# Sliding-window attention into a two-layer network: some transposes moved from TensorE to DMA, and the first steps reordered

## The chip, the cores and the metric

The kernel runs on one core of one Trainium2 chip. The metric is the device time in microseconds of one execution. The profile shows one execution of the program, recorded by the hardware profiler.

Engine names in the views: PE is TensorE's matrix multiplication, PEld its weight load, DVE is VectorE, ACT is ScalarE, POOL is GpSimd, SP is SyncE, which here only issues DMAs. A name such as SPq is the instruction queue of that engine.

## What is computed

```python
batch, n_heads, seq, head_dim = (8, 8, 576, 64)          # q, k, v in float32
n_tokens, d_model, d_ff = (4608, 512, 2048)

# attention: each query sees itself and the 63 keys before it
scores = scale * np.matmul(q, k.transpose(0, 1, 3, 2))
rel = pos[:, None] - pos[None, :]
mask = (rel >= 0) & (rel < 64)
attn = softmax(np.where(mask, scores, -1e9))
attn_out = np.matmul(attn, v)

# heads side by side, then two layers
x = attn_out.transpose(0, 2, 1, 3).reshape(B * S, H * D)   # 4608 x 512
h = x @ w_in
g = h - np.tanh(h)
out = g @ w_out                                            # float32
```

## The kernel before

**Units.** A batch has 576 tokens, that is 9 windows of 64. Two heads make a pair, so a batch has 4 pairs; the number g counts the 32 pairs over all batches (g = 4 b + pair). The two layers work on chunks of 512 tokens, 8 windows, so there are 9 chunks, and a chunk can need windows of two batches: chunk c needs the windows 8c to 8c + 7 of all 72, batch b makes the windows 9b to 9b + 8.

**One pair.** Loads on POOL's queue bring q, k and v of a batch into SBUF and turn them to bf16 on the way; the first loads come in float32 by the queues of ACT and SP. `cast` copies a pair into rows of 128 (two heads side by side), on POOL for most pairs. `tr` transposes 6 such blocks of 96 rows on TensorE into PSUM (L197); the result is copied into `qT` by ACT and VectorE (two copies of 64 partitions) or into `kT` by one copy. `scores` multiplies keys by queries, 9 windows in three groups of three (L210); for the first 8 pairs a second matmul adds the mask (L213). ACT takes the exponential of each group into `PT`. From pair 8 on VectorE multiplies `PT` by the mask (`masking`, L218). `pv` multiplies by v, which has a column of ones for the sum (L224). `norm` divides by that sum on VectorE (L231, L235) and writes `xs`, tokens on partitions. The scores of two heads lie side by side in one matmul, since `qT` holds each head's queries with zeros in place of the other's.

**v.** `cast_v` copies v into `vb`; nine small DMAs (`keys_v`) put each window's keys into the upper 64 partitions of `vw`, and `shift_v` copies them one window on into the lower 64, by VectorE for the first two batches and by one DMA on SP's queue (L135) for the others.

**x.** The layers need x with the model dimension on partitions. `x_tr` transposes 4 or 5 windows of a batch for one half of its heads on TensorE (L241) into PSUM, and ACT or VectorE copies them into `xT`, the tile of a chunk:

```python
o = chunk_tile(c).rearrange("p (h r) (w t) -> p r h w t", r=2, t=64)
```

**The layers.** `hp_mm` multiplies one block of 128 hidden units by the chunk (4 matmuls of 512 columns, L259), ACT takes the tanh (L262), and `g_sub` subtracts it on VectorE and writes `gT` (L268). `yp_mm` multiplies `gT` by `w_out` (L278), 4 matmuls at a time; ACT copies a finished 128 x 512 block and SP stores it (L283, L285).

**The order.** Everything is put on the engines' queues in the order in which the program is written; the engines run their queues in order and wait for one another on semaphores. Slots h order it: an even slot holds one `hp_mm` step, an odd slot one `yp_mm` step, 16 steps behind. After each of them the slot's other work is issued. Chunk c begins at slot 32 c. For the pairs from 12 on this work is laid out by a formula: pair g begins at slot a = 8 g - 48.

```python
at(a - 7, cast, g, "q")
at(a - 5, cast, g, "k")
at(a, tr, g, "q", 3, nc.scalar, nc.vector)
at(a + 2, tr, g, "k", 3, nc.scalar)
for i in range(3):
    at(a + 5 + 2 * i, scores, g, i, 4)
at(a + 11, masking, g)
```

For the first 12 pairs it is written by hand in `PLAN`: a script for each slot, and one (slot -1) for all that goes ahead of the first layer step. A word of a script is a step, its numbers and its engines (a ACT, v VectorE, p POOL, s SP): E and F are `tr` of q and k, a and b their casts, R is a group of scores, P is `pv` with `norm`, M `masking`, X `x_tr` (batch, half of the heads, part), d the cast of v, k `keys_v`, z `shift_v`, q and r loads of one pair, Q, K and V loads of a batch, w and o loads of the weights, i, m and n constants.

**PSUM.** Banks 0 and 1 take the first layer, 2 the second, 3 the transposes, 4 the scores, 5 to 7 the products with v.

Of the kernel before, what the change touches and what calls it, by code (L numbers as in the profile page):

```python
# [7 lines left out]
F32 = mybir.dt.float32  # L8
BF16 = mybir.dt.bfloat16
# [6 lines left out]
def kernel(  # L16
# [9 lines left out]
    nc = tc.nc  # L26
    B, H, S, D = q.shape
    NP = H // 2
    NJ = S // 64
    E, P = 6, S // 6  # L30
# [4 lines left out]
    TOK = 512  # L35
    WPC = TOK // 64
# [4 lines left out]
    ctx.enter_context(tc.manual_schedule())  # L41

    const = ctx.enter_context(tc.tile_pool(name="const", bufs=1))
    qk_pool = ctx.enter_context(tc.tile_pool(name="qk", bufs=2))
    all_pool = ctx.enter_context(tc.tile_pool(name="all", bufs=2))
    v_pool = ctx.enter_context(tc.tile_pool(name="v", bufs=1))
    row_pool = ctx.enter_context(tc.tile_pool(name="row", bufs=3))
    sm_pool = ctx.enter_context(tc.tile_pool(name="sm", bufs=3))
    xt_pool = ctx.enter_context(tc.tile_pool(name="xt", bufs=3))
    g_pool = ctx.enter_context(tc.tile_pool(name="g", bufs=2))  # L50
    psum = ctx.enter_context(tc.tile_pool(name="psum", bufs=1, space=PSUM))


# [10 lines left out]
    NR, NPT = 2, 4  # L64
# [5 lines left out]
    PT = [const.tile([128, NJ, 128], BF16, name=f"pt{i}") for i in range(NPT)]  # L70
    kT = [const.tile([128, 64 + S], BF16, name=f"kt{i}") for i in range(NR)]
    qT = [const.tile([128, 2, S], BF16, name=f"qt{i}") for i in range(NR)]
    xs = [const.tile([128, NJ, NP, D], BF16, name=f"xs{i}") for i in range(2)]

    stage, rows, whole = {}, {}, {}

    def move(eng, o, i):
        if eng is nc.scalar:
            nc.scalar.activation(o, i, ACT.Copy)  # L79
        else:  # L80
            eng.tensor_copy(o, i)  # L81

    def load(g, n, eng):

        b, pr = divmod(g, NP)
        if eng is nc.gpsimd:
            if (b, n) not in whole:
                whole[b, n] = all_pool.tile([P, H, E * D], BF16, tag=n, name=n + "all")
            t = whole[b, n][:, pr::NP]
        else:  # L90
            t = qk_pool.tile([P, 2, E * D], F32, tag=n + "f", name=n + "f")
        eng.dma_start(out=t, in_=(q if n == "q" else k)[b, pr::NP].rearrange("h (p e) d -> p h (e d)", e=E))
        stage[g, n] = t

# [49 lines left out]
    def w_in_tile(ki, m):  # L144
        i = min(m // 4, 2)
        f = 512 * (m // 4 - i) + m % 4
        return w_in_sb[i][:, ki, f:f + 4 * 127 + 1:4]
# [14 lines left out]
    def more_constants():  # L162
        nc.vector.memset(qT[1], 0.0)
        nc.vector.memset(kT[1][:, 0:64], 0.0)
        for i in range(2):
            nc.vector.memset(vw[i][0:64, 0], 0.0)

        for h in range(2):  # L170
            nc.gpsimd.memset(hide[:, h], 0.0)
            nc.gpsimd.affine_select(hide[:, h], hide[:, h], compare_op=ALU.is_ge, fill=-(2.0 ** 30),
                                    base=-1, pattern=[[-1, 64]], channel_multiplier=1)
            nc.gpsimd.affine_select(hide[:, h], hide[:, h], compare_op=ALU.is_ge, fill=-(2.0 ** 30),
                                    base=64, pattern=[[1, 64]], channel_multiplier=-1)
# [9 lines left out]
    xT = {}  # L185

    def chunk_tile(c):
        if c not in xT:
            xT[c] = xt_pool.tile([128, 4, TOK], BF16, tag="xT", name="xT")
        return xT[c]  # L190


    def tr(g, which, bank, *engs):
# [9 lines left out]
        else:  # L203
            move(engs[0], kT[g % NR][:, 64:].rearrange("c (p e) -> c p e", e=E), t)

    def scores(g, grp, bank):
        sp = ps[:, bank, 0:384].rearrange("p (i q) -> p i q", i=3)
        for i in range(3):
            j = 3 * grp + i
            nc.tensor.matmul(sp[:, i, :], kT[g % NR][:, 64 * j:64 * j + 128],  # L210
                             qT[g % NR][:, :, 64 * j:64 * j + 64], start=True, stop=g >= 2 * NP)
            if g < 2 * NP:
                nc.tensor.matmul(sp[:, i, :], ident, hide.rearrange("p h t -> p (h t)"), start=False, stop=True)  # L213
        nc.scalar.activation(PT[g % NPT][:, 3 * grp:3 * grp + 3, :], sp, ACT.Exp, scale=scale)  # L214
# [23 lines left out]
    def x_tr(b, half, w0, w1, bank, eng=nc.vector):  # L238
        tp = ps[:, bank, :].bitcast(BF16)[:, 0:640].rearrange("p (w t) -> p w t", t=128)
        for w in range(w0, w1):  # L240
            nc.tensor.transpose(tp[:, w - w0, :],  # L241
                                xs[b % 2][:, w, 2 * half:2 * half + 2, :].rearrange("p r d -> p (r d)"), ident)
        lo, hi = b * NJ + w0, b * NJ + w1
        while lo < hi:
            c = lo // WPC
            to = min(hi, (c + 1) * WPC)
            o = chunk_tile(c).rearrange("p (h r) (w t) -> p r h w t", r=2, t=64)
            i0 = lo - b * NJ - w0
            move(eng, o[:, half, :, lo - c * WPC:to - c * WPC],
                 tp[:, i0:i0 + to - lo].rearrange("p w (h t) -> p h w t", h=2))  # L250
            lo = to


# [2 lines left out]
    def hp_mm(c, m):  # L256
        hp = ps[:, m % 2, :]
        for ki in range(4):
            nc.tensor.matmul(hp, w_in_tile(ki, m), chunk_tile(c)[:, ki, :],  # L259
                             start=(ki == 0), stop=(ki == 3))  # L260
        th = sm_pool.tile([128, TOK], F32, tag="th", name="th")
        nc.scalar.activation(th, hp, ACT.Tanh)  # L262
        return hp, th
# [27 lines left out]
    def at(h, *fn):  # L291
        items.setdefault(h, []).append(fn)
# [13 lines left out]
    def play(script):  # L306
        for step in script.split():
            what = step[0]
            n = [int(i, 36) for i in step[1:] if i not in "apvs"]
            eng = [ENG[i] for i in step[1:] if i in "apvs"]  # L310
            if what in "qr":
                load(*n, "q" if what == "q" else "k", *eng)
            elif what in "QK":
                load_all(*n, what.lower())
# [41 lines left out]

    PLAN = {
        -1: """
            q0a i v00 a0v v02 v03 v01 d00v d02a r0s b0a r1p q1a E0vv r2p m d03p F0a d01v q3p
            R01 b2a k05s b1a a1v k00s k08a k01p k02a R02 k04a k06s F1a E1vv q2p V1 a2v R00 R12 K1  # L360
            a3p n k07s F2a Q1 k03s z0v w0 d13p w1 K2 E2aa R11 P0 r3s R10 b3a b5p E3va P1
            R21 b6p w2 b4p Q2 d10p F3v a4p R20 d11p R22 P2 V2 d12a k17s k12s k16s k10s R30 k18s
            b7p o3 R32 R31 X001v a7p o2 P3 X010v o0 a5p X000v X011a E4vv a9p b8p""",
        0: "F4a",
        10: "R40 k13s F5v k15s E5aa R42 a6v k14s aAp k11s",
        12: "a8p d20p R41 d23p d21p d22p z1v k24s E6av F6a k27s R50 k25s b9p o1 P4",
        15: "R51 R52 R61 F7a k22s P5 R62 bAp R60 E7va",
        16: "k21p",
        19: "bBp P6 X100a R71 k20s k28s F8a k23s k26s R70",
        20: "R72 E8vv",  # L370
        23: "X101a z2s R80 E9aa P7 R81",
        26: "F9a R82 X111a X110a",
        31: "R90 EAvv",
        35: "M8 R92 FAa aBv R91 FBa M9 RA2",
        41: "P9 RA0 EBaa",
        44: "P8 RB0",
        50: "RA1 MA X200a RB1 X201v PA RB2",
        56: "MB PB",
        60: "X210v",
        62: "X211a",  # L380
# [4 lines left out]

    for g in range(3 * NP, B * NP):
        b, pr = divmod(g, NP)
        a = 8 * g - 48
        at(a - 7, cast, g, "q")
        at(a - 5, cast, g, "k")  # L390
        at(32 * b - 72 + 5 * pr, cast_v, b, pr)
        at(a, tr, g, "q", 3, nc.scalar, nc.vector)
        at(a + 2, tr, g, "k", 3, nc.scalar)
        for i in range(3):
            at(a + 5 + 2 * i, scores, g, i, 4)
        at(a + 11, masking, g)
        for i in range(3):
            at(a + 13 + i, pv, g, i)
        at(a + 15, norm, g)
        if pr % 2 == 1:  # L400
            at(a + 20, x_tr, b, pr // 2, 0, 4, 3)
            at(a + 22, x_tr, b, pr // 2, 4, NJ, 3)
        for j in range(NJ):
            if pr == 0:
                at(32 * b - 54 + j // 2, keys_v, b, j)
        if pr == 0:
            at(32 * b - 78, load_v_all, b)
            at(32 * b - 64, load_all, b, "q")
            at(32 * b - 63, load_all, b, "k")
            at(32 * b - 47, shift_v, b, 0, NJ - 1)  # L410

    LAG = 16
    for h in range(min(items), 2 * (16 * NC + LAG) + 2):
        n = h // 2
        c, m = divmod(n, M)
        cy, sy = divmod(n - LAG, M)
        if h % 2 == 0:
            if sy % 4 == 0 and 0 < n - LAG <= 16 * NC:
                y_out(*divmod((n - LAG) // 4 - 1, 4))
            if 0 <= c < NC:  # L420
                hidden = hp_mm(c, m)
        elif 0 <= cy < NC:
            yp_mm(cy, sy)
        for fn in items.get(h, []):
            fn[0](*fn[1:])
        if h % 2 == 0 and 0 <= c < NC:
            g_sub(c, m, *hidden)
# [29 lines left out]
```

The softmax here doesn't subtract the row's maximum and nothing guards it: scores larger than these inputs give would overflow.

## Time and profile before

| | |
|---|---|
| time, median of 11 runs | 363.42 us (361.31 to 366.63) |
| the profiled execution: time | 362.93 us |
| the profiled execution: span from first to last instruction | 361.2 us |
| mean granted TensorE clock | 0.993 |
| busy: TensorE, VectorE, ScalarE, GpSimd | 323.4, 215.3, 192.8, 103.8 us |
| DMA | 36.76 MB, mean 102 GB/s |
| first layer: 552 matmuls recorded | 146.2 us, 382 ns each |
| second layer: 559 matmuls recorded | 143.0 us, 379 ns each |
| transposes of q, of k, of x on TensorE | 192, 192, 144 matmuls; 14.4, 14.7, 13.1 us |

In the rows of the page and of the views below, a group's row gives the line in the kernel, the engine, the operation, output and inputs by their names, the shape and the number of instructions. The time of a matmul in the trace runs from its start to its modelled end, and matmuls overlap, so that start-to-start distances say what one costs. The slices of the page are 40 equal parts of the span, about 9 us each, with the busy share in tenths.

### The profile page before, as it was taken

How to read it: one execution, taken by the hardware profiler on the slowest of the kernel's cores; microseconds unless marked ns; L12 is line 12 of the kernel's file. 1: busy time of each engine (PE TensorE's matmuls, PEld its weight loads, DVE VectorE, ACT ScalarE, POOL GpSimd, SP SyncE). 2: the span in 40 equal slices, each digit the busy share in tenths (PEclk: the TensorE clock that was granted, in tenths of full speed). 3: DMA queues.
4: the chain of work that ended last, by engine and by line, in shares of the span. 5: the costliest groups of instructions: out<-in, count | busy, mean ns of one | idle time of the engine just before them, and what ended most of it. 6: DMA issues, size and time to landing. Idle time of an engine off the chain costs nothing.

```text
span 361.2 us, 6002 instructions
## 1 busy us (share of the span) xinstructions
PE 323.4 (90%) x2288; PEld 189.0 (52%) x2329; DVE 215.3 (60%) x352; ACT 192.8 (53%) x355; POOL 103.8 (29%) x136
## 2 busy tenths in 40 slices
PE   0528687889999999999999999999999999999995
PEld 0427345655555555555555555555555544444442
DVE  4317667865676776767777767767666633443300
ACT  3435366876566656565655565655664444444421
POOL 7708353806318408402730372110000000000000
PEclk9999899999999999999999999999999999999999
DMA  8899993467876576755935591250000010010012
GB/s 163 138 214 186 214 221 64 59 132 133 196 141 92 89 164 112 148 104 127 136 79 112 135 138 54 62 123 31 30 32 29 31 58 29 31 58 29 31 68 78
DMA packets 31948, 36.76 MB, mean 102 GB/s; under 512 B 3472, under 2 KB 25872, under 8 KB 31536
## 3 DMA queue, kind: packets, MB, share of 16 engines
q0 software_dynamic: 20384, 17.90, 32.9%
q1 hardware_dynamic: 10904, 17.69, 17.0%
q10 hardware_dynamic: 632, 0.79, 0.7%
q8 instruction: 18, 0.29, 0.3%
q14 instruction: 10, 0.08, 0.1%
HBM read 36.70 MB, written 9.44 MB: 128 GB/s over the span
## 4 chain that ended last, share of the span: by engine, by line
PE 78%; DMA 8%; DVE 6%; ACT 3%; issue 2%; SPq 2%; ACTq 0%; DVEq 0%
PE ps L278 33%; PE ps L259 30%; DMA vw<-vb 6%; PE ps L224 5%; PE ps L197 4%; PE ps L210 4%; DVE xs L235 2%; PE ps L241 2%; SPq L127 2%; ACT th L262 1%; DMA qf<-in_q_dram 1%; DVE qt L81 1%; DMA vw<-vw 1%; ACT pt L214 1%; DVE gT L268 1%
## 5 line engine op out<-in xcount | busy, mean ns | idle before, releaser
L259 PE MATMUL ps<-xT,wi 128*128 128x512 bf16 x552 | 146.2, 382 | 2.6 <-DVE gT L268 1.3
L278 PE MATMUL ps<-w_out_sb,gT 128*128 128x512 bf16 x559 | 143.0, 379 | 1.1 <-ACT ysb L283 0.2
L268 DVE TENSOR_TENSOR gT<-ps,th 128x512 bf16<-128x512 f32 x144 | 99.0, 690 | 75.3 <-ACT th L262 74.2
L262 ACT ACTIVATE th<-ps 128x512 f32<-128x512 f32 x144 | 86.0, 598 | 82.8 <-PE ps L259 80.4
L259 PEld LDWEIGHTS <-wi 128*128 128x128 bf16 x576 | 61.3, 114 | 47.5 <-issue 3.3
L278 PEld LDWEIGHTS <-gT 128*128 128x128 bf16 x576 | 53.6, 98 | 51.3 <-issue 0.5
L214 ACT ACTIVATE pt<-ps 128x384 bf16<-128x384 f32 x96 | 46.9, 491 | 50.7 <-PE ps L210 37.7
L81 POOL COPY vb<-vall 72x1024 bf16<-72x1024 bf16 x28 | 29.4, 1063 | 71.3 <-DMA vw<-vb 42.4
L235 DVE TENSOR_TENSOR xs<-ps,rc 64x576 bf16<-64x576 f32 x64 | 48.3, 755 | 1.5
L210 PE MATMUL ps<-qt,kt 128*128 128x128 bf16 x288 | 36.7, 228 | 6.9 <-ACT pt L214 3.3
L224 PE MATMUL ps<-vw,pt 128*128 128x130 bf16 x288 | 30.0, 228 | 8.5 <-DVE vw L133 6.8
L224 PEld LDWEIGHTS <-pt 128*128 128x128 bf16 x288 | 22.5, 102 | 22.4 <-issue 8.3
L81 POOL COPY qb<-qall 96x768 bf16<-96x768 bf16 x27 | 22.9, 847 | 34.1 <-PE ps L197 21.5
L81 DVE COPY qt<-ps 64x576 bf16<-64x576 bf16 x33 | 25.0, 758 | 12.7 <-ACT qt L79 8.3
L81 POOL COPY kb<-kall 96x768 bf16<-96x768 bf16 x28 | 23.7, 848 | 29.7 <-DMA kall<-in_k_dram 10.7
L210 PEld LDWEIGHTS <-kt 128*128 128x128 bf16 x288 | 24.6, 103 | 11.7 <-ACT kt L79 3.4
L283 ACT ACTIVATE ysb<-ps 128x512 f32<-128x512 f32 x36 | 21.4, 594 | 15.1 <-PE ps L278 15.1
L81 DVE COPY xT<-ps 128x512 bf16<-128x512 bf16 (+4 forms) x35 | 12.1, 368 | 16.8 <-PE ps L241 16.8
L79 ACT ACTIVATE kt<-ps 128x576 bf16<-128x576 bf16 x30 | 19.4, 646 | 3.7 <-issue 2.1
L79 ACT ACTIVATE qt<-ps 64x576 bf16<-64x576 bf16 x31 | 19.7, 635 | 2.5 <-DVE qt L81 1.5
L197 PE MATMUL ps<-ident,qb 96*128 96x96 bf16 x192 | 14.4, 215 | 6.9 <-DVE qb L81 6.7
L197 PE MATMUL ps<-ident,kb 96*128 96x96 bf16 x192 | 14.7, 217 | 4.8 <-ACT kb L79 3.7
(47 smaller groups left out, 148.0 us busy)
## 6 DMA issues: line engine op xcount, KB each, us to landing
out_dram<-ysb SPq DMA_DIRECT2D x36, 256.0 KB
vw<-vb SPq DMA_DIRECT2D x67, 65.0 KB
vall<-in_v_dram POOLq DMA_DIRECT2D x7, 576.0 KB, 9.2
kall<-in_k_dram POOLq DMA_DIRECT2D x7, 576.0 KB, 9.1
qall<-in_q_dram POOLq DMA_DIRECT2D x7, 576.0 KB, 6.7
vw<-vw SPq DMA_DIRECT2D x6, 520.0 KB
w_out_sb<-in_moe_w_out_dram POOLq DMA_DIRECT2D x4, 512.0 KB, 11.1
wi<-in_moe_w_in_dram POOLq DMA_DIRECT2D x2, 512.0 KB, 14.3
```

Of the source, the lines that this page charges most:

```text
L79: nc.scalar.activation(o, i, ACT.Copy)
L81: eng.tensor_copy(o, i)
L197: nc.tensor.transpose(tp[:, e, :], src[:, e, :], ident[:P, :P])
L210: nc.tensor.matmul(sp[:, i, :], kT[g % NR][:, 64 * j:64 * j + 128], qT[g % NR][:, :, 64 * j:64 * j + 64], start=True, stop=g >= 2 * NP)
L214: nc.scalar.activation(PT[g % NPT][:, 3 * grp:3 * grp + 3, :], sp, ACT.Exp, scale=scale)
L224: nc.tensor.matmul(ps[:, 5 + grp, 130 * i:130 * i + 130], PT[g % NPT][:, j, :], vw[b % 2][:, j, 2 * pr:2 * pr + 2, :], start=True, stop=True)
L235: nc.vector.tensor_tensor(xo[r, :, :, pr, :], ov[r, :, :, h, 0:D], rc[r].to_broadcast([64, 3, 3, 64]), ALU.mult)
L259: nc.tensor.matmul(hp, w_in_tile(ki, m), chunk_tile(c)[:, ki, :], start=(ki == 0), stop=(ki == 3))
L262: nc.scalar.activation(th, hp, ACT.Tanh)
L268: nc.vector.tensor_tensor(gT[c][:, m, :], hp, th, ALU.subtract)
L278: nc.tensor.matmul(yp, gT[c][:, m, s * 128:(s + 1) * 128], w_out_sb[:, m, :], start=(m == 0), stop=(m == M - 1))
L283: nc.scalar.activation(ysb, ps[:, yp_bank(c, s), :], ACT.Copy)
```

## The change

x of the batches from 3 on (counted from 0) is transposed by DMA: `x_dma`, called once a batch, 16 slots after its last pair begins, issues on SP's queue one or two transposing DMAs from `xs` straight into the tiles of the chunks. The tile of a chunk has another order for it, window by window, and the first layer reads it in 8 runs of 64 columns. `x_tr` stays for the batches 0 to 2.

k of the batches from 4 on is transposed by DMA: `cast2` casts two pairs side by side into one tile, `bounce` writes it to scratch in DRAM, `tr2` reads it back transposing into `kT2`. The load of k goes 5 slots earlier, and the pairs of batch 4 begin 2 slots earlier, those from batch 5 on 4 slots.

The scripts of the first steps have a new order. The float32 loads of q and k share one set of three buffers.

```diff
-    qk_pool = ctx.enter_context(tc.tile_pool(name="qk", bufs=2))
+    qk_pool = ctx.enter_context(tc.tile_pool(name="qk", bufs=3))
...
+    two_pool = ctx.enter_context(tc.tile_pool(name="two", bufs=1))
+    dram = ctx.enter_context(tc.tile_pool(name="dram", bufs=2, space=bass.MemoryType.DRAM))
...
+    kT2 = [const.tile([128, 2, 64 + S], BF16, name=f"kt2{i}") for i in range(2)]
...
-            t = qk_pool.tile([P, 2, E * D], F32, tag=n + "f", name=n + "f")
+            t = qk_pool.tile([P, 2, E * D], F32, tag="f", name=n + "f")
...
+        for i in range(2):
+            nc.vector.memset(kT2[i][:, :, 0:64], 0.0)
...
-            xT[c] = xt_pool.tile([128, 4, TOK], BF16, tag="xT", name="xT")
+            xT[c] = xt_pool.tile([128, WPC, 2, 128], BF16, tag="xT", name="xT")
...
+    def cast2(g):
+
+        if g % 2 == 0:
+            two[g // 2] = two_pool.tile([P, E, 2, 2, D], BF16, tag="k", name="kb2")
+        nc.gpsimd.tensor_copy(two[g // 2][:, :, g % 2].rearrange("p e h d -> p h e d"),
+                              stage.pop((g, "k")).rearrange("p h (e d) -> p h e d", d=D))
+
+    def bounce(i):
+        t = dram.tile([S, 256], BF16, tag="k", name="kd")
+        nc.sync.dma_start(out=t.rearrange("(p e) c -> p (e c)", e=E),
+                          in_=two[i].rearrange("p e i h d -> p (e i h d)"))
+        two[i] = t
+
+    def tr2(i):
+        nc.sync.dma_start(out=kT2[i % 2][:, :, 64:], in_=two.pop(i), transpose=True)
+
     def scores(g, grp, bank):
+        kt = kT[g % NR] if g < 4 * NP else kT2[g // 2 % 2][:, g % 2]
...
-            o = chunk_tile(c).rearrange("p (h r) (w t) -> p r h w t", r=2, t=64)
             i0 = lo - b * NJ - w0
-            move(eng, o[:, half, :, lo - c * WPC:to - c * WPC],
-                 tp[:, i0:i0 + to - lo].rearrange("p w (h t) -> p h w t", h=2))
+            move(eng, chunk_tile(c)[:, lo - c * WPC:to - c * WPC, half, :], tp[:, i0:i0 + to - lo])
+            lo = to
+
+    def x_dma(b):
+        lo, hi = b * NJ, (b + 1) * NJ
+        while lo < hi:
+            c = lo // WPC
+            to = min(hi, (c + 1) * WPC)
+            nc.sync.dma_start(out=chunk_tile(c)[:, lo - c * WPC:to - c * WPC].rearrange("p w r t -> p (w r) t"),
+                              in_=xs[b % 2][:, lo - b * NJ:to - b * NJ].rearrange("p w r d -> p (w r d)"),
+                              transpose=True)
             lo = to
...
-            nc.tensor.matmul(hp, w_in_tile(ki, m), chunk_tile(c)[:, ki, :],
+            nc.tensor.matmul(hp, w_in_tile(ki, m),
+                             chunk_tile(c)[:, :, ki % 2, 64 * (ki // 2):64 * (ki // 2) + 64],
...
-            q0a i v00 a0v v02 v03 v01 d00v d02a r0s b0a r1p q1a E0vv r2p m d03p F0a d01v q3p
-            R01 b2a k05s b1a a1v k00s k08a k01p k02a R02 k04a k06s F1a E1vv q2p V1 a2v R00 R12 K1
-            a3p n k07s F2a Q1 k03s z0v w0 d13p w1 K2 E2aa R11 P0 r3s R10 b3a b5p E3va P1
-            R21 b6p w2 b4p Q2 d10p F3v a4p R20 d11p R22 P2 V2 d12a k17s k12s k16s k10s R30 k18s
-            b7p o3 R32 R31 X001v a7p o2 P3 X010v o0 a5p X000v X011a E4vv a9p b8p""",
+            q0a r0s i a0v v00 v02 v03 d02a d00v b0a v01 q1a E0vv r1p d01v r2p m d03p b1v F0a
+            k00s q3p k08a a1v R01 F1v R02 E1vv b2a k01p k02a k04a q2p k05s V1 R00 K1 k03s Q1 a2v
+            n k06s F2a R10 k07s z0v R12 a3p r3s E2aa P0 d11p d13p w0 R11 w1 E3aa R22 b3a R21
+            b5p w2 Q2 P1 K2 R20 d10p a5p F3v d12a k17s a4p P2 k16s R31 k10s b4p X001v V2 a7p
+            k18s R30 b7p o2 k12s k13s X000a R32 b6p P3 o3 k15a X010v X011a E4vv""",
         0: "F4a",
-        10: "R40 k13s F5v k15s E5aa R42 a6v k14s aAp k11s",
-        12: "a8p d20p R41 d23p d21p d22p z1v k24s E6av F6a k27s R50 k25s b9p o1 P4",
-        15: "R51 R52 R61 F7a k22s P5 R62 bAp R60 E7va",
-        16: "k21p",
-        19: "bBp P6 X100a R71 k20s k28s F8a k23s k26s R70",
+        10: "a6v o0 R40 a9p aAp E5aa k14s b8p F5v a8p R42",
+        12: "k11s d20p d22p R41 F6a d21p d23p z1v k25s k27s E6aa R50 P4",
+        15: "b9p R52 o1 k24p k22s k20s R51 R61 F7a P5 R62 E7aa",
+        19: "R60 F8a k23s R71 P6 k21p k28s X100a k26s R70",
...
-        a = 8 * g - 48
+        a = 8 * g - 48 - (0, 2, 4)[min(b - 3, 2)]
+        s = 32 * b - (0, 2, 4)[min(b - 3, 2)]
         at(a - 7, cast, g, "q")
-        at(a - 5, cast, g, "k")
-        at(32 * b - 72 + 5 * pr, cast_v, b, pr)
+        if b < 4:
+            at(a - 5, cast, g, "k")
+        elif pr % 2 == 0:
+            at(a - 14, cast2, g)
+            at(a - 13, cast2, g + 1)
+            at(a - 11, bounce, g // 2)
+            at(a - 5, tr2, g // 2)
+        at(s - 72 + 5 * pr, cast_v, b, pr)
         at(a, tr, g, "q", 3, nc.scalar, nc.vector)
-        at(a + 2, tr, g, "k", 3, nc.scalar)
+        if b < 4:
+            at(a + 2, tr, g, "k", 3, nc.scalar)
...
-        if pr % 2 == 1:
-            at(a + 20, x_tr, b, pr // 2, 0, 4, 3)
-            at(a + 22, x_tr, b, pr // 2, 4, NJ, 3)
+        if pr == NP - 1:
+            at(a + 16, x_dma, b)
...
-            at(32 * b - 78, load_v_all, b)
-            at(32 * b - 64, load_all, b, "q")
-            at(32 * b - 63, load_all, b, "k")
-            at(32 * b - 47, shift_v, b, 0, NJ - 1)
+            at(s - 78, load_v_all, b)
+            at(s - 64, load_all, b, "q")
+            at(s - (63 if b < 4 else 68), load_all, b, "k")
+            at(s - 47, shift_v, b, 0, NJ - 1)
```

The scripts of the slots from 20 to 50 have small changes of the same kind, which are left out here.

## The prediction, made before the changed kernel ran

> **What bounds the kernel now.** I read the page from the engine shares to the 40 slices, then busy time by stage, the order of TensorE's instructions in time, and the chain of waits. The rows of engine shares and of slices:
>
> ```profile
> PE 323.4 (90%) x2288; PEld 189.0 (52%) x2329; DVE 215.3 (60%) x352; ACT 192.8 (53%) x355; POOL 103.8 (29%) x136
> PE   0528687889999999999999999999999999999995
> DMA  8899993467876576755935591250000010010012
> ```
>
> TensorE is full from the tenth slice to the end; the DMA engines are full only in the first six. Busy time by stage (engines in the order PE, PEld, DVE, ACT, POOL; then clock, DMA share, GB/s):
>
> ```profile
> 0.00:40.00 40.00, 16.78 (x166) 14.33 (x167) 18.79 (x34) 15.68 (x25) 24.33 (x42) 1.00 1.05 179
> 40.00:100.00 60.00, 51.88 (x452) 32.78 (x458) 41.32 (x66) 39.78 (x78) 26.11 (x31) 0.97 0.75 142
> 130.00:300.00 170.00, 168.53 (x1201) 97.63 (x1224) 116.03 (x193) 97.70 (x183) 40.70 (x48) 1.00 0.41 87
> ```
>
> From 130 to 300 us TensorE idles 1.5 us of 170, with DVE at 68% and ACT at 57%. There a TensorE instruction that disappears is worth its start-to-start time. In the first 40 us TensorE idles 23 us, in the next 60 it idles 8: those stages hang on waits. The timeline of TensorE (start us, us):
>
> ```profile
> 135.23 0.42 PE L197 MATMUL ps<-ident,kb 96*128 96x96 bf16 x6
> 135.49 1.03 PE L278 MATMUL ps<-w_out_sb,gT 128*128 128x512 bf16 x4
> ...
> 145.76 0.39 PE L241 MATMUL ps<-ident,xs 128*128 128x128 bf16 x4
> 145.98 1.03 PE L278 MATMUL ps<-w_out_sb,gT 128*128 128x512 bf16 x4
> ...
> 148.05 0.44 PE L241 MATMUL ps<-ident,xs 128*128 128x128 bf16 x5
> 148.32 0.33 PE L224 MATMUL ps<-vw,pt 128*128 128x130 bf16 x3
> ```
>
> Durations overlap, so starts decide: six k transposes hold TensorE for 135.49 - 135.23 = 0.26 us (not 6 x 0.217), x transposes for 0.22 and 0.27 us. Last, two stretches of the chain of waits (start us, us):
>
> ```profile
> 9.81 0.49 DVE vw L166
> 10.30 0.29 DVE vb L81
> ...
> 14.63 11.22 DMA vw<-vb
> ...
> 26.59 1.57 DVE vw L133
> ...
> 82.44 4.26 DMA vw<-vw
> ```
>
> The start hangs on the key copies of v into `vw`, which land 11 us after issue behind a software ring that is 99.9% busy from 10 to 45 us. The last line is the nearest row for what is added: an SBUF-to-SBUF transfer of 520 KB on SP's queue, 4.3 us to landing.
>
> **The change part by part, against the profiled execution (span 361.2, time 362.93, so 1.7 around it; the median of the runs shown is 0.5 above it).**
>
> *Removed from TensorE.* k: batches 4 to 7, 16 pairs x 0.26 = 4.2 us. x: batches 3 to 7, two halves each, 10 x (0.22 + 0.27) = 4.9 us. Together 9.1 us, all in the full stretch. ACT loses 16 evacuations of kT at 0.646 us (10.3 us), ACT and DVE those of xT; both lie beside TensorE: zero.
>
> *Who is late next.* Two pairs now take 17.59 us (first-layer matmuls at 132.11 and 149.70, 16 slots): 1.10 a slot. They will take (17.59 - 0.52 - 0.49)/16 = 1.04. DVE rises to 68% x 1.10/1.04 = 72% at most. Waits of TensorE for `g_sub` total 1.3 us in before; I add none.
>
> *The moving operand of the first layer* becomes 8 runs of 64 elements. Scores read their operand in runs of 64 too: three start 0.17 us apart from the next group, as do three of `pv` with 130 in a row. So zero; 5% of 576 x 0.216 would be 6 us.
>
> *Added on POOL:* `cast2` does the same casts (0.83 us each), two together and earlier. k loads go out 6 slots (6.2 us) ahead of their cast, where they landed in 9.1: POOL waits 2.9 us, with the q casts behind it, each planned 7 slots (7.3 us) ahead. Zero.
>
> *Added on SP's queue:* 8 bounces, 8 `tr2`, 10 transposes of x (two a batch), for the same key copies and stores. No transposing DMA is in the trace. Below: no cost, as all is issued ahead of need. Above: as follows. SP runs in order. `x_dma` stands 16 slots after the batch's last pair starts and waits for DVE's `norm`, about 1.5 slots more. Right behind it on the same ring stands `tr2` of the next batch's second two pairs, whose scores come 9.5 slots later (batches 3, 4: 9.8 us) or 11.5 (batches 5, 6: 11.9 us). So 18 blocks of 128x128 for x and 9 for k plus about 2 us of issue and landing must fit: 27p + 2 <= 9.8, or p <= 0.29 us a block. For chunk 3 alone, 10 blocks + 2 must fit into 6.5 slots (6.8 us): p <= 0.48. The 2 us are from the trace: the key copies before the shift at 134.68 were issued until 132.79 and had landed when it went.
>
> What is p? A block is 128 rows of 256 B, 8 packets on each of 16 engines. By the `vw` shift, 4.3 us for 532,480 B gives 32,768 B in 0.26 us, landing included. A page speaks against the change: the Trainium skill, "VectorE: DVE Perf Modes", "The three transpose paths", puts a 128x128 bf16 transpose at 390 ns on TensorE and 1309 ns by DMA, and its rules take TensorE if PSUM will do. In the trace TensorE spends 0.055 us a block, so DMA is dearer. If 1.31 us a block were throughput, 162 blocks (90 x, 72 k) would take 212 us in the 139 slots (144 us) from the first `tr2` to the last `x_dma`: about 68 us longer, 421 in place of 353. "DMA: Bandwidth & Descriptors", "Latency and other measured facts", has 261 GB/s for a transposing DMA: 0.126 us a block. I read the 1.31 as one small transfer with its fixed part and take p between 0.13 and 0.26, by the shift row. Then 27p + 2 is 5.4 to 9.0 us: it fits. Software loads share the ring time (28% of the engines from 130 to 250 us), and k of batch 5 is issued in the very slot of the first `x_dma`, so I allow 1 us of stalls in all; ends 0 and 75.
>
> *The bounce* goes out 6 slots before `tr2` (6.2 us): 288 KB in rows of 3 KB, against 4.3 us for 520 KB. Covered; if late, it adds to the same wait.
>
> *First steps.* The vb cast that gates the key copies (10.30) now comes before the 1.6 us of memsets. The fourth v load must have landed; v casts started about 1 us apart (6.37, 7.30, 8.35), so some 9.4. POOL's cast ends at 9.41. Copies start about 0.8 us earlier; ends 0 and 1.2. X000, alone between 40.69 and 41.59 before the first-layer matmuls at 42.06, moves ahead of P3: 0.9 us; ends 0 and 0.9. w0 leaves POOL's queue after two v casts that wait for V1 (26.4 us): issued at about 29, not 16.5. The ring is full until then and keeps its order (Q1 lands at 33.3), so w0 still lands near 35, needed at 40; if it took its 18.5 us from issue, 47: 6 us late. One key copy moves to ACT's queue (0.9 to 2.3 us of issue), where ACT was idle for 4.4 us before its copy of X011. k's second cast and copy go from ACT to DVE, which idled 3.1 us there. The new memsets take 0.1 us each. The moved steps from slot 10 on keep their instructions among 8 us of TensorE idle: zero, ends -2 and 2. In all -1.7.
>
> *Sum:* 361.2 - 9.1 - 1.7 + 1.0 = 351.4 span, + 1.7 = 353.1; I say 353.0, 2.9% under the median.
>
> **The rivals.** A (forecast): transposes land in time; 348 to 357 with the ends of first steps and stalls. For it: DMA share 0.41 in the stretch that pays.
>
> B, part of it is given back: w0 late (up to +6), or p near 0.32, so that each of four batches waits about a microsecond: 357 to 361.
>
> C, slower: transposes are slow, and the second `tr2` behind `x_dma` on SP becomes the wait of every batch. Stall per batch 27p - 7.8 (batches 3, 4) or 27p - 9.9 (5, 6). At p = 0.48 (8 packets at the 60 ns which the 1040 B packets of the key copies take) these are 5.2 and 3.1, 16.6 in all, against 10.8 gained: 369 with my allowance left out. It decides from p = 0.43, where the four stalls (3.8, 3.8, 1.7, 1.7) eat the gain; at 1.31 it is 421. For it: small packets and shared rings. Against it: the shift row.
>
> D, nothing moves: DVE or ACT holds the slot at 1.10 us; 361 to 363. Against it: 72%.
>
> **How the numbers follow.** A 0.67, B 0.12, C 0.17, D 0.04. Runs of this kernel spread by 0.7% either way; about 0.5% (1.8 us) is what a measurement can tell from no change. Faster: A and all but the end of B, 0.78; same: D and that end, 0.05; slower: C, 0.17. Range 347.5 to 363: A with its lower ends, B and D; left out are C and a few per cent below. A's own range is 348 to 357.
>
> **What would show it.** Right: 186 transposes fewer on TensorE; TensorE idle still under 3 us from 130 to 290; two pairs in 16.6 us; first-layer matmuls starting near 40.4 us. Wrong: TensorE waiting at the scores for DMA kt2, or at the first layer of chunks 3 and 4 for DMA xT; packets of the transposes above 50 ns; first-layer groups of four longer than 0.86 us; first-layer matmuls starting after 42 us.

## The result, and the profile after

| | before | after |
|---|---|---|
| time, median | 362.88 us (47 runs) | 358.77 us (12 runs, 354.1 to 362.29) |
| ratio | 1 | 0.9853 [0.9827, 0.9879] |
| profiled execution: span, time | 361.2, 362.93 us | 356.9, 358.76 us |
| mean granted TensorE clock | 0.993 | 0.989 |

Faster by 1.5%, where the forecast was 2.9%. Ratios, here and below, leave out runs over 1.5% above the fastest of the same kernel (3 of the 12), while the medians have all runs, by which it is 1.1%. The profiled execution has the median's time, so its trace can be read for the difference. From the page, the rows of shares and slices:

```profile
PE 317.1 (89%) x2112; PEld 180.7 (51%) x2143; DVE 204.1 (57%) x324; ACT 187.3 (52%) x340; POOL 103.8 (29%) x138
PE   0539787999899999599999999999999999999995
PEclk9999899999999999989999999999999999999999
DMA  8998997659849769967997799556100410010011
```

By the groups of the trace, 96 transposes of k and 90 of x have gone from TensorE, the 186 of the prediction. But the row of slices, in before all nines from the tenth slice to the last but one, has a 5 in the middle (the 17th slice, 142.8 to 151.7 us). The clock row has an 8 in the slice after it. The DMA row is mostly at 6 to 9 from the eighth to the 25th slice, where it was mostly at 3 to 7. Busy time by stage (PE, PEld, DVE, ACT, POOL; then clock, DMA share, GB/s):

```profile
0.00:40.00 40.00, 19.16 (x181) 16.90 (x182) 19.33 (x38) 15.80 (x26) 26.32 (x45) 0.98 0.97 166
130.00:290.00 160.00, 152.40 (x973) 83.38 (x991) 103.87 (x162) 86.77 (x158) 38.96 (x46) 0.99 0.69 132
```

TensorE idles 7.6 us of the 160, where it idled 1.5 us of 170. The same view in steps of 5 us finds the place:

```profile
140.00:145.00 5.00, 4.66 (x34) 2.50 (x33) 3.39 (x7) 1.98 (x4) 0.00 (x0) 1.00 1.15 173
145.00:150.00 5.00, 1.77 (x15) 0.95 (x14) 2.83 (x4) 2.31 (x5) 4.11 (x5) 1.00 1.34 138
150.00:155.00 5.00, 3.82 (x10) 1.46 (x11) 1.26 (x2) 0.60 (x1) 1.85 (x3) 0.66 1.03 242
155.00:160.00 5.00, 5.00 (x40) 2.93 (x39) 2.33 (x5) 2.20 (x5) 2.50 (x3) 1.00 0.52 89
```

From 145 to 150 us TensorE is busy for 1.77 us of 5. In the stretch in which it comes back its granted clock is 0.66, and it starts 10 matmuls, where 40 follow in the next. While it waits, the DMA share is above 1 (more than one transfer under way at each DMA engine), and yet only 138 GB/s move. What it waits for stands at the end of each line of TensorE's timeline (start us, us, then the idle time before and its releaser). These are the ones after 130 us with more than 0.25 us:

```profile
141.93 0.34 PE L249 MATMUL ps<-vw,pt 128*128 128x130 bf16 x3 [0.34 <-DVE pt L243]
...
151.18 1.90 PE L292 MATMUL ps<-xT,wi 128*128 128x512 bf16 x4 [4.35 <-DMA xT<-xs]
...
180.74 0.34 PE L249 MATMUL ps<-vw,pt 128*128 128x130 bf16 x3 [0.70 <-DVE pt L243]
...
220.53 1.05 PE L292 MATMUL ps<-xT,wi 128*128 128x512 bf16 x4 [0.46 <-DMA xT<-xs]
```

The first matmuls of chunk 3 (L292 is the first layer now) wait 4.35 us for the first x that DMA transposes, and then take 1.90 us, not the 1.03 of a group of four at full clock. The next group is as slow, and the clock is at half for just these two:

```profile
152.87 1.91 PE L312 MATMUL ps<-w_out_sb,gT 128*128 128x512 bf16 x4
```

```profile
151.23:154.65 3.42, 3.42 (x9) 1.23 (x10) 0.91 (x2) 0.60 (x1) 0.84 (x2) 0.50 1.01 268
```

Two smaller waits are for masked scores (L243). SP's queue and GpSimd's in those microseconds:

```profile
138.81 0.35 SPq L319 DMA_DIRECT2D out_dram<-ysb  x1
140.51 7.85 SPq L281 DMA_TRANSPOSE xT<-xs  x2
148.41 2.56 SPq L228 DMA_TRANSPOSE kt<-kd  x1
```

```profile
135.14 0.77 POOL L102 DMA_DIRECT2D kall<-in_k_dram  x1
...
136.89 0.77 POOL L102 DMA_DIRECT2D qall<-in_q_dram  x1
...
145.89 0.82 POOL L218 COPY kb<-kall 96x768 bf16<-96x768 bf16 x1 [8.23 <-DMA kall<-in_k_dram]
```

GpSimd put the k and q loads of batch 5 (576 KB each) on the software ring 5.4 and 3.6 us ahead of SP's first transposes, though the order of the program has k's load in the same slot and q's four slots behind: GpSimd runs ahead of the slots, while `x_dma` must wait for `norm`. SP then needs 7.85 us to issue two transposing DMAs. In the trace's DMA packets, the first transposing packet runs at 145.09, 4.6 us after SP began to issue. The store that SP issued ahead of them, at 138.81, has its first packet at 143.33, 4.5 us later: all that SP issued stood still, not the transposes alone. From 139 to 146 us the software ring moves 160 to 200 packets of 768 B a microsecond. The transposing packets come at 170 to 330 a microsecond from 146 to 150 us, beside the rest of the loads, and at some 790 and then 1120 a microsecond once the loads have landed.

To place every microsecond I use the lead: the start of a chunk's first tanh in before, minus that in the kernel at hand, each in its profiled execution. (The experiments' columns are explained below.)

| chunk | changed kernel | e5, first steps alone | e8, without loads | e10, no shift | e11, no shift, ordered |
|---|---|---|---|---|---|
| 2 | 2.97 | 3.61 | 3.74 | 3.83 | 4.29 |
| 3 | -2.35 | 3.60 | 3.80 | 4.08 | 4.55 |
| 4 | -2.34 | 3.59 | 4.29 | -1.35 | 6.58 |
| 5 | -0.53 | 3.59 | 6.75 | -6.26 | 8.62 |
| 6 | 1.70 | 3.58 | 9.20 | -6.06 | 10.66 |
| 7 | 4.22 | 3.58 | 11.72 | -4.54 | 12.18 |

The changed kernel enters chunk 2 with 3 us of lead, has lost 5.3 by the start of chunk 3, gains nothing within chunk 3 (e8 gains only 0.5 there), and then 1.8, 2.2 and 2.5 in the chunks after it. At chunk 8 the lead is still 4.22, so the last two chunks, which read x in 8 runs of 64 columns, pay nothing for that.

### The profile page after: what moved, and what is told of

The parts are those of the page before. It is cut to its first block, busy times and chain, and to the rows that moved or that the text cites. A ratio compares the mean times of both kernels' runs of the same rounds, so it can differ in the third digit from the quotient of the medians.

```text
span 356.9 us, 5601 instructions
## 1 busy us (share of the span) xinstructions
PE 317.1 (89%) x2112; PEld 180.7 (51%) x2143; DVE 204.1 (57%) x324; ACT 187.3 (52%) x340; POOL 103.8 (29%) x138
## 4 chain that ended last, share of the span: by engine, by line
PE 73%; DMA 9%; ACT 6%; DVE 5%; issue 2%; POOL 2%; SPq 1%; ACTq 0%; DVEq 0%; POOLq 0%
PE ps L312 32%; PE ps L292 30%; PE ps L249 4%; PE ps L235 4%; DMA xT<-xs 3%; DMA vw<-vb 3%; PE ps L203 2%; ACT th L296 2%; DVE xs L260 2%; DMA kt<-kd 2%; DVE gT L302 2%; DMA vall<-in_v_dram 1%; ACT pt L239 1%; SPq L131 1%; ACT qt L83 1%
## 5 line engine op out<-in xcount | busy, mean ns | idle before, releaser
L292 PE MATMUL ps<-xT,wi 128*128 128x512 bf16 x576 | 149.3, 383 | 6.0 <-DMA xT<-xs 4.8
L312 PE MATMUL ps<-w_out_sb,gT 128*128 128x512 bf16 x545 | 140.7, 381 | 2.4 <-ACT ysb L317 0.8
L292 PEld LDWEIGHTS <-wi 128*128 128x128 bf16 x576 | 61.0, 114 | 52.8 <-DMA xT<-xs 5.5
L312 PEld LDWEIGHTS <-gT 128*128 128x128 bf16 x576 | 54.6, 98 | 59.3 <-issue 3.0
L235 PE MATMUL ps<-qt,kt 128*128 128x128 bf16 x288 | 37.5, 230 | 7.3 <-ACT pt L239 6.3
L85 DVE COPY qt<-ps 64x576 bf16<-64x576 bf16 x30 | 22.7, 758 | 14.7 <-ACT qt L83 13.3
L218 POOL COPY kb<-kall 96x768 bf16<-96x768 bf16 x16 | 13.1, 828 | 37.0 <-DMA kall<-in_k_dram 21.0
L83 ACT ACTIVATE qt<-ps 64x576 bf16<-64x576 bf16 x34 | 21.6, 636 | 1.7 <-PE ps L203 1.6
L243 DVE TENSOR_TENSOR pt<-pt,ps 128x1152 bf16<-128x1152 bf16 x24 | 17.9, 744 | 0.4 <-ACT pt L239 0.4
L203 PEld LDWEIGHTS <-qb 96*128 96x128 bf16 x192 | 12.2, 104 | 9.8 <-DVE qb L85 6.2
L238 PE MATMUL ps<-hide,ident 128*128 128x128 bf16 x72 | 13.7, 263 | 0.0
```

What stands on the lines that cost most here:

```text
L203: nc.tensor.transpose(tp[:, e, :], src[:, e, :], ident[:P, :P])
L235: nc.tensor.matmul(sp[:, i, :], kt[:, 64 * j:64 * j + 128], qT[g % NR][:, :, 64 * j:64 * j + 64], start=True, stop=g >= 2 * NP)
L292: nc.tensor.matmul(hp, w_in_tile(ki, m), chunk_tile(c)[:, :, ki % 2, 64 * (ki // 2):64 * (ki // 2) + 64], start=(ki == 0), stop=(ki == 3))
L312: nc.tensor.matmul(yp, gT[c][:, m, s * 128:(s + 1) * 128], w_out_sb[:, m, :], start=(m == 0), stop=(m == M - 1))
```

## The experiments

**First set: is it the loads, the place of x of batch 3, k or x?** (before on that chip: 362.17)

e1 moves the loads of q and k of batches 5 to 7 ahead, so that they don't meet `x_dma`:

```diff
-            at(s - 64, load_all, b, "q")
-            at(s - (63 if b < 4 else 68), load_all, b, "k")
+            at(s - (64 if b < 5 else 81), load_all, b, "q")
+            at(s - (63 if b < 4 else 68 if b < 5 else 84), load_all, b, "k")
```

> Loads of k and q of batches 5 to 7 issued 16 and 17 slots earlier; all else as in the changed kernel. Theory (the software loads of k and q of batch 5, issued just ahead of the first transposes of x, share the DMA engines and hold these up): the 4.4 us wait of chunk 3 for xT goes, and with it the drop of the TensorE clock behind it (about 1.5 us more): 352.5 us, transposing packets of batch 3 all within 4 us of their issue. Rival 1 (a transposing DMA of 10 blocks is slow in itself, its issue on SP alone takes 4.9 us): the wait stays above 3 us, 358 us. Rival 2 (norm of batch 3 is late): the issue is late, the wait stays, 358 us.

Measured: 355.62 us (353.77 to 357.95), ratio 0.9818 [0.9771, 0.9865]. The wait for xT is gone. A new one has come, from TensorE's timeline:

```profile
134.01 0.34 PE L235 MATMUL ps<-qt,kt 128*128 128x128 bf16 x3 [2.58 <-DMA kt<-kd]
```

The moved loads now meet the first `tr2`: its 1152 packets took from 125.77 to 133.15, with a mean of 53 ns, where they took 2.6 us in the changed kernel. The collision was moved, not removed; the interval overlaps that of the changed kernel.

e2 leaves x of batch 3 on TensorE:

```diff
-        if pr == NP - 1:
+        if b == 3 and pr % 2 == 1:
+            at(a + 20, x_tr, b, pr // 2, 0, 4, 3)
+            at(a + 22, x_tr, b, pr // 2, 4, NJ, 3)
+        if b > 3 and pr == NP - 1:
             at(a + 16, x_dma, b)
```

> x of batch 3 transposed on TensorE again, from batch 4 on by DMA. Theory: the wait of chunk 3 goes (5.9 us with the clock), two halves of TensorE transposes come back (1.0 us): 353.9 us; no other wait for xT above 0.5 us, since later batches need fewer blocks and have more slots. Rival 1 (transposes slow in themselves): the wait moves to chunk 4 (8 blocks) with 2 to 4 us: 357 us.

Measured: 352.9 us (352.1 to 354.45), ratio 0.9754 [0.9728, 0.978]: with two transposing DMAs fewer it is 1% faster than the changed kernel. No wait for xT or kt2 is left. What is left in the stretch, beside the two waits for masked scores, are transposes of q waiting for the copy that empties PSUM bank 3, which `x_tr` shares with them now that the pairs of batch 4 begin 2 slots earlier:

```profile
125.69 0.42 PE L203 MATMUL ps<-ident,qb 96*128 96x96 bf16 x6 [0.47 <-DVE xT L85]
...
145.41 0.42 PE L203 MATMUL ps<-ident,qb 96*128 96x96 bf16 x6 [1.13 <-DVE xT L85]
```

e3 keeps all x on TensorE (k alone by DMA: `x_tr` as in e2, for every batch, and no `x_dma`), e4 keeps all k on TensorE (x alone by DMA: `cast`, `tr` and `kT` as in before for every batch). Both keep the shift of the pairs.

> Only k by DMA; x of all batches on TensorE. Theory: 4.9 us of TensorE transposes come back, the wait of chunk 3 goes with its 5.9 us: about 1 us less than the changed kernel, 357.8 us, and no wait for kt2. Rival (the path of k through DRAM is what costs): a wait for kt2 or for the casts on POOL stays, 361 us or more.

> Only x by DMA; k of all batches on TensorE. Theory (the software loads are the cause; k's scratch and transposes have little part in it): 4.2 us come back and the wait of chunk 3 stays at 3 to 5 us: 362.5 us. Rival (k's bounce and transposes on SP's queue hold x up): the wait goes, 357 us.

Measured: e3 360.03 us, ratio 0.9931 [0.9908, 0.9954]; e4 355.44 us (354.29 to 359.41), ratio 0.9829 [0.9772, 0.9887]. e3 loses to the collisions in bank 3 seen in e2, now in batch after batch: 0.48, 1.13, 0.41 and 1.08 us. With the two waits for masked scores that is 4.1 us, as much as k's transposes had given back. The profiled run of e4, at 359.41 the slowest of its four, has the xT wait at chunk 3, of 2.44 us, without any `tr2` on SP's queue. So `tr2` behind `x_dma` is not what makes the first x late. e4's median came out below what I expected; I can't say from its one trace whether its other runs had the wait.

**Second set: the size of the parts.** (before on that chip: 363.09)

e5 is before with the scripts of `PLAN` and the shared q and k buffers of the changed kernel, and nothing else.

> The kernel before with the new scripts of the first steps alone (all transposes on TensorE, old formula). Theory (the new first steps are worth 1.9 us, by the start of the first layer at 40.1 instead of 42.1 us): 360.4 us. Rival (their gain lies only in the state of the DMA engines from run to run, and the mean is no better): 362.2 us.

Measured: 358.97 us (358.36 to 359.73), ratio 0.9892 [0.9861, 0.9924]: 4.1 us by the medians, over twice the 1.7 of the prediction. The lead in its trace is 3.6 us from chunk 1 on and stays there. The stage of the layers is full, as in before:

```profile
130.00:290.00 160.00, 159.80 (x1165) 92.24 (x1164) 110.89 (x185) 92.67 (x174) 40.68 (x48) 1.00 0.42 87
```

So of the changed kernel's 1.5%, some 1.1% is the new order of the first steps. The 186 transposes that went to DMA brought about 0.4% more (0.9853 / 0.9892 = 0.996), and the two intervals overlap; the medians of all runs, 358.77 and 358.97, are even alike.

The lead begins early. TensorE's last `pv` of the first pair, in e5:

```profile
25.42 0.59 PE L224 MATMUL ps<-vw,pt 128*128 128x130 bf16 x4 [0.82 <-DVE vw L133]
```

and the same in before:

```profile
28.20 0.59 PE L224 MATMUL ps<-vw,pt 128*128 128x130 bf16 x4 [0.89 <-DVE vw L133]
```

That is 2.8 us of the 3.6, before 29 us, at the first use of the key copies of v.

e6 is e2 with `x_tr` of batch 3 one slot earlier (a + 19 and a + 21), out of the way of q. e7 is e6 with k on TensorE as in e4: x of the batches from 4 on is all that DMA transposes.

> As e2, with the TensorE transposes of x of batch 3 one slot earlier, so that they no longer share a slot and PSUM bank 3 with the q transposes of batch 4, which begin 2 slots earlier in the changed kernel. Theory (the idle of 0.5 and 1.1 us before those q transposes in e2 is that collision): both gaps go, 351.5 us. Rival (they only move to the next instruction): 352.9 us.

> Only x by DMA and only from batch 4; k on TensorE throughout; batch 3 spaced as in e6. Theory (each removed set counts by its TensorE time): e6 plus 4.2 us of k transposes, 355.7 us. Rival (k's detour pays for itself only in part, through POOL, SP and the software ring): 353 to 354 us.

Measured: e6 353.44 us (351.66 to 353.94), ratio 0.973 [0.9694, 0.9767]; e7 354.92 us (353.7 to 355.47), ratio 0.9773 [0.9736, 0.9811]. The gaps in front of q are gone in e6, but its time can't be told from that of e2. Between e6 and e7 lies k's detour, 1.5 us by the medians with intervals that just overlap, where 4.2 us of transposes leave TensorE.

e8 is the changed kernel with what was suspected taken out: no q or k is loaded for batches 5 to 7.

```diff
+        if b < 5:
             t = all_pool.tile([P, H, E * D], BF16, tag=n, name=n + "all")
             nc.gpsimd.dma_start(out=t, in_=(q if n == "q" else k)[b].rearrange("h (p e) d -> p h (e d)", e=E))
+            last[n] = t
+        t = last[n]
```

> The changed kernel without the loads of q and k of batches 5 to 7; these batches use the tiles of batch 4 again, so that part of the input is left out. Theory (software loads hold the transposes up): no wait for xT or kt2, each x_dma with its tr2 done within 5 us of issue, 352.5 us. Rival (the transposing DMA is slow by itself or stands behind a store on SP's ring): the wait of chunk 3 stays at 3 us or more, 357 us.

Measured: 350.9 us (350.09 to 351.26), ratio 0.9666 [0.9638, 0.9694]. All waits for DMA are gone; of TensorE's gaps after 130 us the two for masked scores are left, 0.34 and 0.70. SP issues the two transposes in a third of the time, and the 3456 packets of the first `x_dma` with its `tr2` ran from 140.96 to 145.49:

```profile
139.75 2.86 SPq L286 DMA_TRANSPOSE xT<-xs  x2
```

Those 27 blocks in 4.5 us are 0.17 us a block, inside the 0.13 to 0.26 of the prediction. A store stands ahead of them on SP's queue here as well, issued at 138.05, and has its first packet after 0.8 us, so the store was not the cause. The loads are what made them late, then: but this run leaves the loads out, and shows that they cost time, not how to have both.

**Third set: is the shift of the pairs needed?** The 0.34 and 0.70 us stand where the shift steps from 0 to 2 and from 2 to 4 slots and two pairs come 6 slots apart instead of 8. e9 and e10 are e6 with shifts (0, 2, 2) and (0, 0, 0) in place of (0, 2, 4). (before on that chip: 362.71)

> As e6, with the pairs from batch 5 on beginning 2 slots earlier instead of 4, so that the second place where two pairs stand 6 slots apart instead of 8 is gone. Theory (the wait of pv for the masked scores, 0.7 us near 175 us in e6 and the changed kernel, is that place): this wait goes and no transpose is late, 352.6 us. Rival (the lead of 2 slots is needed by transposes beside the loads): a wait for xT at chunk 5 or for kt2 of 1 us or more, 354 us or more.

> As e6 without any shift of the pairs of batches 4 to 7. Theory (the lead pays for the transposes beside the software loads): the 0.3 and 0.7 us waits for the masked scores go, but chunk 4, whose x then has 6.5 slots (6.7 us) for 8 blocks, waits 1 us or more for xT: 353.5 to 355 us. Rival (with batch 3 on TensorE all transposes have lead enough): 352 us.

Measured: e9 366.11 us (361.89 to 370.33), ratio 1.0051 [1.0021, 1.008]; e10 365.26 us (362.45 to 368.18), ratio 1.0066 [1.0041, 1.0092]. I had expected both within 3 us of e6; they lose 12. The two waits for masked scores are gone as expected, but TensorE's timeline of e10 has this at the starts of chunks 4 and 5:

```profile
185.35 1.89 PE L292 MATMUL ps<-xT,wi 128*128 128x512 bf16 x4 [5.76 <-DMA xT<-xs]
...
225.42 1.90 PE L292 MATMUL ps<-xT,wi 128*128 128x512 bf16 x4 [4.51 <-DMA xT<-xs]
```

and the granted clock is 0.50 in the 5 us after each (185 to 190 and 225 to 230). SP's queue and GpSimd's show the pattern of the changed kernel again, a k load 2.2 us ahead of the transposes and a q load 0.4 us ahead:

```profile
173.05 9.08 SPq L281 DMA_TRANSPOSE xT<-xs  x2
```

```profile
170.87 0.77 POOL L102 DMA_DIRECT2D kall<-in_k_dram  x1
...
172.62 0.77 POOL L102 DMA_DIRECT2D qall<-in_q_dram  x1
```

In e6 the same k load is issued at 167.89 and the transposes at 174.28, 6.4 us apart, and chunk 4 begins at 182.48, 8.2 us after the transposes were issued, with 0.17 us of waiting. In e10 chunk 4 would have begun 6.5 us after the issue (185.35 - 5.76 - 173.05), and could begin after 12.3. Two things differ, then: how far the loads are ahead, and how much lead the chunk has. So either the slots of lead decide, or what is on the rings at that moment. That was the last question.

**Fourth set: all loads, but in order.** e11 is e10, e12 is the changed kernel, each with a tie from the transposes to the loads, in e11 for batches 6 and 7, in e12 for batches 5 to 7 (`if b >= 5`). (before on that chip: 362.75)

```diff
+    def gate(b):
+        w = (b + 1) * NJ - 1
+        nc.gpsimd.tensor_copy(mark, chunk_tile(w // WPC)[0:1, w % WPC, 0, 0:2])
...
+            if b >= 6:
+                at(s - 68, gate, b - 2)
             at(s - 64, load_all, b, "q")
```

> The version without a shift (x of batch 3 on TensorE; 365.3 us, with waits of TensorE for xT of 5.8 us at chunk 4 and 4.5 us at chunk 5), with one more step: before the k load of batches 6 and 7, GpSimd copies two elements of the x that was transposed for the batch two before, so that the loads start only when those transposes have landed. Theory (the transposes are late only because the software loads run on the same rings): both waits for xT go, SP issues those transposes in about 3 us instead of 9, and the time falls by their 10.3 us and the clock lost with them to about 353, a ratio of 0.97 to 0.98. Rival (the lead in slots is what counts, since the transposes are long after norm anyway): the waits stay at 4 us or more and the time stays above 362. Second rival: the loads, now 5 us later, make k of the same batch late (waits for kt2 or for POOL's casts): 357 to 362.

> The changed kernel with the same step before the k loads of batches 5, 6 and 7 (behind x of batches 3, 4 and 5), nothing else moved. Theory: the 4.4 us wait for xT at chunk 3 goes, and with it the clock loss and the lateness of chunk 3; a time of 351 to 353.5, ratio 0.968 to 0.975, as in the version that left these loads out (350.9). Rival: k of batch 5, loaded about 6 us later, is late for its cast and its second pair of transposes, a wait for kt2 of 2 us or more near 160 us, and the time is 355 to 358.

Measured: e11 351.38 us (350.64 to 352.55), ratio 0.9684 [0.9661, 0.9707]; e12 353.76 us (352.48 to 359.37), ratio 0.9755 [0.9719, 0.979]. One copy of two elements ahead of two k loads takes e10 from 365.3 to 351.4 us, with no slot of lead added. SP's queue of e11 at the same place:

```profile
171.91 2.77 SPq L282 DMA_TRANSPOSE xT<-xs  x2
174.78 1.45 SPq L229 DMA_TRANSPOSE kt<-kd  x1
```

GpSimd's timeline of e11 has the copy, and the loads right behind it:

```profile
177.28 0.17 POOL L292 COPY mark<-xT 1x2 bf16<-1x2 bf16 x1 [7.63 <-DMA xT<-xs]
177.40 0.77 POOL L103 DMA_DIRECT2D kall<-in_k_dram  x1
```

and on its page the first layer waits for no DMA at all (idle before it, last column: 1.1 us):

```profile
L297 PE MATMUL ps<-xT,wi 128*128 128x512 bf16 x576 | 148.4, 381 | 1.1 <-DVE gT L307 1.0
```

GpSimd stands still for 7.6 us in front of the copy, and nobody misses it: k and q still come in time. e11 does all the work and is within 0.5 us of e8, which left the loads out. So the lead in slots is needed only where the loads collide with the transposes; without the collision the kernel does without the shift, and without its two waits for masked scores. (That e11 is faster than e12 does not show this alone, since they also differ in x of batch 3 and in the order of the loads of batch 5.) In e12 the wait for xT is gone too. One part of its rival shows: the cast of q stands behind the later cast of k on GpSimd, and a transpose of q waits for it:

```profile
153.81 0.43 PE L204 MATMUL ps<-ident,qb 96*128 96x96 bf16 x6 [1.05 <-POOL qb L86]
```

That, a wait of 0.46 us for the shifted v near 208 us, and the two waits for masked scores are what e12 has and e11 has not. e11 is the fastest complete version, faster than both kernels: 0.9684 against 0.9853.

## Why the prediction was right and wrong

The sign was right, and the time is in the range; but 358.8 us lies in the stretch of rival B (part of it given back), not in the forecast's own 348 to 357, and it was given back in another way than B had it: by one wait of 4.4 us and what follows from it, not by a microsecond in each batch; and w0, issued at 28.70 us, kept no matmul waiting. That it fell into the range at all is in part luck, as two errors of the sum have opposite signs. By the terms of the sum, for the span of the profiled execution:

| term | predicted | measured |
|---|---|---|
| transposes off TensorE | -9.1 | -9.0 |
| first steps | -1.7 | -3.0 |
| stalls | +1.0 | +7.8 |
| sum | -9.8 | -4.2 |

- **Transposes off TensorE: right.** In e8 the lead grows from 3.74 at chunk 2 to 11.72 at chunk 7, 8.0 us, and 1.04 us of waits for masked scores lie within: 9.0. To cost them by start-to-start distance was right; DVE did not become the bound.
- **First steps: half of what they bring.** The lead of the changed kernel at chunk 2 is 2.97, that of e5 3.6. In the changed kernel the first layer starts at 40.06 us, as predicted (40.4), against 42.06 in before. About a microsecond more comes from the clock, which the sum left out: it is 0.50 for the first 3.4 us of the layer in before (42.08 to 45.49 us), but from 38.59 to 42.01 in the changed kernel, so that the second hidden block already runs at full clock there, and the lead goes from 1.54 at the first tanh to 2.50 at the second (in e5 from 3.15 to 4.18). The moved steps from slot 10 on, taken as zero with ends of 2 us either way, then give 0.4 in the changed kernel and take 0.6 in e5. In e5 the first layer starts at 38.47, and the key copies, issued 0.9 us earlier as predicted (0.8), had been of use 2.8 us earlier. Which of the moved steps does it was not tried one by one and stays open.
- **Stalls: the step that failed.** 2.97 + 9.02 gained, less the 4.22 kept, leaves 7.8. From the trace: 4.35 + 0.46 waiting for xT, 0.34 + 0.70 for masked scores, and 1.75 for the two groups of four after the wait, which took 1.90 and 1.91 instead of 1.03: 7.6, all but 0.2. The prediction had seen the place ("k of batch 5 is issued in the very slot of the first `x_dma`"), but gave it 1 us, for a share of the ring time. It took the price of a block, which is right alone (0.17), and the 28% of the software ring, as if the rings were shared by time. In the runs the transposes issued just behind the loads did not start for 3.6 to 5.3 us, and in the changed kernel ran at a third of their rate until the loads had gone. The 2 us for issue and landing were 4.6 us to the first packet alone. The trace of before already had such a delay, in a plain store on the same queue, issued behind loads of q and k:

```profile
141.44 0.77 POOL L98 DMA_DIRECT2D kall<-in_k_dram  x1
```

```profile
141.86 0.34 SPq L285 DMA_DIRECT2D out_dram<-ysb  x1
```

Its first packet runs at 145.02, 3.2 us after the issue. The stores at 115.73, 177.02 and 212.19, behind loads as well, wait 3.2 to 3.7 us; the one at 150.90, with no load under way, 0.8. With these 3.2 to 3.7 us in place of the 2, and 0.26 us a block, ten blocks take an estimated 5.8 to 6.3 of the 6.8 us that chunk 3 leaves them: next to no margin.
- **10 blocks fit if p is under 0.48:** right as a formula, and right in e8 and e12, where no load was under way beside the ten blocks. A budget of time against time needed the other user of the resource in it, and when it comes; GpSimd ran up to 5 us ahead of its slots, so the slots did not tell.
- **The shift's own price** (two pairs 6 slots apart, 1.04 us of masked scores that VectorE brought late) was not looked for.
- **The sign for it, packets above 50 ns, was a poor one:** all transposing packets of the changed kernel together have a median of 18 and a mean of 28 ns. The 1280 of the ten late blocks do have a mean of 55 (median 31), but 4.6 us of the delay lie ahead of the first of them. The other sign, TensorE waiting for xT at chunk 3, was the right one to look at.
- **1.31 us a block** (the Trainium skill, "VectorE: DVE Perf Modes", "The three transpose paths"), which would have made the kernel 68 us slower, was rightly not taken as throughput: 27 blocks took 4.5 us.
- **k:** 4.2 us was expected of it; e6 against e7 gives 1.5, not well separated from zero. But from chunk 2 to 7 the lead grows by 7.9 us in e11 and by 3.9 in e7 (4.21 to 8.13), which transposes only x of the same batches by DMA. So where no transfer is late, k is worth about the 4.0 us between them. (e7 has the shift too, and a wait of 0.46 us from it.)
- **The sum:** its two errors, +6.8 and -1.3, partly cancel, and the total looks better than its parts.

## What to carry to other kernels

In this kernel a DMA on SP's queue, a store or a transposing one, had its first packet 3.2 to 5.3 us after the issue, not 0.8 or 1.2, at the places measured here where it was issued just behind the loads of q and k on the software ring. If such a transfer is due soon, make the loads depend on its landing (here by a copy of two elements), rather than start everything earlier, which moved the collision to the next transfer (e1). A store in the trace of the kernel before can show the delay: compare its issue with its first packet. When a transfer is costed against its deadline, list what else is on the DMA engines in that window, by the time at which each engine really issues it, since an engine whose queue is free runs ahead of the program's order. And time each part of a composite change alone: here the part that looked incidental, the order of the first steps, brought most of the gain.

## What the hardware showed that was not expected

- **SP's transfers give way to the loads, at first entirely.** Two transposing DMAs of x take SP 2.8 us to issue without loads on the rings (e8, e11) and 7.0 to 9.1 us just behind them (changed kernel, e6, e10). The first packet came 1.2 us after the issue at the places shown of e8 and e11, and 3.6 to 5.3 us after it in the changed kernel (batches 3 and 5), e6 and e10 (batches 4 and 5), where the loads had begun to move 0.6 to 3.9 us before. It is not the mere presence of a load: x of batch 4 in the changed kernel, issued at 179.33, 6.8 us after the loads had begun to move, started after 1.2 us, while q's load ran until 182.0. Whether the packets wait for descriptors or for their turn at the DMA engines the traces do not tell; that part stays open.
- **A wait costs more than itself, and a short one as much.** After waits of 4.35, 5.76 and 4.51 us the next group of four matmuls took 1.89 to 1.90 us; the granted clock was 0.50 for 3.4 us in the changed kernel and for 6.8 us each time in e10. Waits of 2.58 us (e1), 2.44 (e4), 3.05 and 2.43 (e9) were each followed by 3.4 us at 0.50 too, in e4 from 0.75 us after the wait on. In the layers' stage, waits up to 1.15 us (e1) were not. The Trainium skill, "TensorE: Matmul & The Clock Gate", "Part 1: The HAM clock gate", halves the clock after an idle window of about 3.4 us. Here TensorE had been busy for up to 0.98 us of the 3.4 us before the clock fell (e4), so that less than a whole idle window was enough.
- **The start varies by itself.** With the same first steps the first tanh starts anywhere between 38.0 (e2) and 42.0 us (changed kernel) in the profiled runs. The clock is part of it: in e2 it is 1.00 from the first matmul of the layer on, in the changed kernel 0.50 for the first 1.95 us. A difference of under 1% between two single runs says nothing here.
